# Making the first pair's attention operands on the engines and putting them ahead of the second pair's, in an attention and soft-MoE kernel

## The chip, the core and the metric

One core of a Trainium2 chip. Times are device microseconds (us) of one execution. The core's engines are TensorE (PE, with its weight load PEld), VectorE (DVE), ScalarE (ACT), GpSimd (POOL) and SyncE (SP); ACT, POOL and SP also issue DMAs, which the profile writes as ACTq, POOLq and SPq. All the DMAs run on 16 shared DMA engines.

## The reference

```python
q_n, k_n = rmsnorm(q, g_q), rmsnorm(k, g_k)         # x / sqrt(mean(x*x) + 1e-6) * g, over D = 64
scores = (q_n @ k_n.T) / sqrt(D)                    # 4 batches, 12 heads, 448 rows
attn = softmax(scores) @ v                          # 1792 rows of 768
x = (relu(attn @ w_in) ** 2) @ w_out                # 768 -> 2048 -> 768, weights in 64-bit floats
logits = x @ phi                                    # 8 experts of 4 slots
slot_input = softmax(logits, over rows).T @ x
slot_out[e] = relu(slot_input[e] @ w1[e]) @ w2[e]   # 768 -> 1024 -> 768
out = softmax(logits, over slots) @ slot_out
```

## The kernel before

Attention works on 24 pairs of heads, six to a batch. While it goes on, the 64-bit weights of the first layer are fetched in 32 pieces of 768 KB (`fetch64`, on GpSimd's DMA queue), turned into 32-bit floats on ACT and DVE (`convert`: tiles `top`, `wf`, `wh`), and stored to scratch memory on SP's queue (`wi_s`, `wo_s`); the first layer's products for a finished batch (`ph`) fill TensorE's gaps. After attention come the last batch's first layer and the experts, whose weights SP streams in.

The code is written as blocks (`load`, `norm`, `trans0`, `trans1`, `max0`, `row0`, `s00`, `v00` and so on), which `attention` calls in the sequence of `ORDER`, each with its distance in pairs ahead of the scores. A scheduler then puts every engine's instructions in one fixed order; an engine takes them strictly in that order, and one that waits holds everything behind it on that engine or queue.

What happens to one pair, with the tile names:

- `load` brings q and k of both heads (`qk`). It has four buffers, two per pair, so that the loads of pair 2 wait until pair 0's `norm` has read its own, and those of pair 3 until pair 1's has.
- `norm` squares both on ACT (`sq`, one buffer), sums on DVE (`ss`), makes the inverse root by a first guess on ACT (`y`, L245) and three Newton rounds of three small DVE steps (L247 to L249), and multiplies (`qs`, L261).
- `trans` turns q and k over on TensorE into PSUM (`pm`) and makes the operands of each head. `m1` is q rounded to the matmul format, on 64 partitions, and again on the other 64; `m2` is what the rounding left, and row 64 of `m2` holds minus the row maximum. `s1` is k times the gains `gkq`, rounded, with its residue on the other 64 partitions; `s2` is the rounded part again. ACT writes the rounded halves, DVE the residues, and the two second copies (`m1` to `m1`, `s1` to `s2`) are made by DMA: pair 0's on ACT's queue (`small`), the others' on SP's. The profile cuts numbers off, so that `m<-m` is the copy of `m1`, and `m<-mt` the write of the row maxima.
- `rowmax` multiplies `s1` with `m1` and takes the maximum on DVE (`nm`), `maxrow` turns it over, copies it (`mt`) and sends it by DMA into row 64 of `m2`. `scores` does the two products that make the final scores; of the first pair `s00` and `s01` belong to head 0. `values` multiplies with v (`pv`).

Three sets of `m1`, `m2`, `s1`, `s2` go round among the heads. Ahead of the first pair stand `gains` (the product of g_q, g_k and the scale, one DVE instruction that waits for four small loads on ACT's queue) and, in the code of the same time, `selectors` (constant tiles `i4`, `r4`, `i4h`, `seln`, `sel4`, some 13 small DVE instructions). `gate` is a DVE instruction that holds the first weight conversion back until pair 0's last operand is made.

Of the kernel before, what the change touches and what calls it, by code (L numbers as in the profile page):

```python
# [20 lines left out]
def raw(ap):  # L21
    return ap.bitcast(F32)
# [19 lines left out]
VF, PD, LEAD, SLOPE = 9, 4, 1.5, 0.75  # L42
WF, EARLY, NTOP = 4, 1, 1
LAG, GATE, MTQ = 1, 1, 1


ON_PL = [1, 0, 1, 1, 1, 1, 1, 1, 1, 1, 1, 0, 1, 0, 0, 1]
# [12 lines left out]
def tile_attention_moe_softmoe(  # L60
# [22 lines left out]
    nc = tc.nc  # L83
# [20 lines left out]
    make_identity(nc, ident)  # L104
    gkq = const.tile([128, 1], F32, tag="gkq", name="gkq")
    gq2 = const.tile([128, 1], F32, tag="gq2", name="gq2")
    i4 = const.tile([128, 32], F32, tag="i4", name="i4")
    r4 = const.tile([128, 4, 32], F32, tag="r4", name="r4")
    i4h = const.tile([128, 2, 32], F32, tag="i4h", name="i4h")
# [93 lines left out]
    def load_v(t):  # L203
        b, hp = divmod(t, NP)
        vh, vl = vst[t % 2]
        if t < VF:
            vf = att.tile([CP, 2, NC, D + 1], F32, tag="vr", name=f"vf_{t}", bufs=2)
            nc.vector.memset(vf[:, :, :, D:], 1.0)
            live[t]["vf"] = vf
            for j in range(2):  # L210
                nc.sync.dma_start(
                    vf[:, j, :, :D], v[b, 2 * hp + j].rearrange("(p c) d -> p c d", c=NC)
                )
            return
        vr = att.tile([CP, 2, NC, D + 1], F32, tag="vr", name=f"vr_{t}", bufs=2)
        vr = vr.rearrange("p h c d -> p (h c d)")[:, : 2 * NC * D].rearrange("p (h c d) -> p h c d", h=2, c=NC)
        nc.sync.dma_start(
            vr.rearrange("p h c d -> p h (c d)"),
            v[b, 2 * hp : 2 * hp + 2].rearrange("h (p c) d -> p h (c d)", c=NC),
        )  # L220
        for j in range(2):
            nc.scalar.copy(vh[:, j, :, :D], vr[:, j])
        for j in range(2):
            nc.vector.tensor_tensor(vl[:, j], vr[:, j], raw(vh[:, j, :, :D]), ALU.subtract)
# [6 lines left out]
    def inverse_rms(ts):  # L231
        n = 16 * len(ts)
        ss = att.tile([CP, 32], F32, tag="ss", name=f"ss_{ts[0]}", bufs=1)[:, :n]
        for x, t in enumerate(ts):
            for i in range(2):
                sq = att.tile([CP, 8, D], F32, tag="sq", name=f"sq_{t}_{i}", bufs=1)
                qf = live[t]["qk"][i].rearrange("p h c d -> p (h c) d")
                nc.scalar.activation(sq, qf, AF.Square)  # L238
                at = 16 * x + 8 * i
                nc.vector.tensor_reduce(ss[:, at : at + 8], sq, AX.X, ALU.add)  # L240
        ms = att.tile([CP, 32], F32, tag="ms", name=f"ms_{ts[0]}", bufs=1)[:, :n]
        y = att.tile([CP, 32], F32, tag="y", name=f"y_{ts[0]}", bufs=2)[:, :n]
        u = att.tile([CP, 32], F32, tag="u", name=f"u_{ts[0]}", bufs=1)[:, :n]
        nc.vector.tensor_scalar(ms, ss, 1.0 / D, EPS, ALU.mult, ALU.add)
        nc.scalar.activation(y.bitcast(I32), ms.bitcast(I32), AF.Copy, bias=float(0x5F3759DF), scale=-0.5)  # L245
        for _ in range(3):
            nc.vector.scalar_tensor_tensor(u, y, -0.5, y, ALU.mult, ALU.mult)  # L247
            nc.vector.tensor_tensor(u, u, ms, ALU.mult)
            nc.vector.scalar_tensor_tensor(y, u, 1.5, y, ALU.add, ALU.mult)  # L249
        for x, t in enumerate(ts):  # L250
            live[t]["y"] = y[:, 16 * x : 16 * x + 16]

    def norm(t):
        ts = together(t)
# [20 lines left out]
    def trans(t, i):  # L275
# [6 lines left out]
        for j in range(2):  # L282
            o = operands(t, j)
            src = ps[64 * j : 64 * j + 64, :S]
            if i == 0:
                nc.scalar.copy(o["m1"][0:64, :], src)
                small(t).dma_start(raw(o["m1"][64:128, :]), raw(o["m1"][0:64, :]))
                nc.vector.tensor_tensor(o["m2"][0:64, :], src, raw(o["m1"][0:64, :]), ALU.subtract)
            else:
                g = gkq[64 * j : 64 * j + 64, :]  # L290
                nc.scalar.activation(o["s1"][0:64, :], src, AF.Copy, scale=g)
                small(t).dma_start(raw(o["s2"][0:64, :]), raw(o["s1"][0:64, :]))
                nc.vector.scalar_tensor_tensor(
                    o["s1"][64:128, :], src, g, raw(o["s1"][0:64, :]), ALU.mult, ALU.subtract
                )
                if GATE and t == 0 and j == 1:
                    gate(raw(o["s1"][0:1, 0:1]))
# [5 lines left out]
    def gains():  # L303
        for half in range(2):
            nc.scalar.dma_start(gkq[64 * half : 64 * half + 64, :], g_k.rearrange("(d o) -> d o", o=1))
            nc.scalar.dma_start(gq2[64 * half : 64 * half + 64, :], g_q.rearrange("(d o) -> d o", o=1))
        nc.vector.scalar_tensor_tensor(gkq, gkq, scale, gq2, ALU.mult, ALU.mult)

    def selectors():
        nc.sync.dma_start(phi_sb, phi.rearrange("(kc p) s -> p kc s", p=128))  # L310
        nc.vector.tensor_tensor(i4, ident[:, 0:32], ident[:, 32:64], ALU.add)
        nc.vector.tensor_tensor(i4, i4, ident[:, 64:96], ALU.add)
        nc.vector.tensor_tensor(i4, i4, ident[:, 96:128], ALU.add)
# [122 lines left out]
    def attention():  # L436
        for t in range(-3, NT + 1):
            for key in ORDER:
                dt, cost, run = blocks[key]
                if 0 <= t + dt < NT:  # L440
                    run(t + dt)
                    if t == -3:
                        gains()
                        for u in units[:PD]:
# [697 lines left out]
```

## Time and profile before

| | |
|---|---|
| Median of 3 runs | 835.5 us (829.1, 835.5, 840.67) |
| The profiled execution | 825.38 us, of which the span of its instructions is 823.4 us |
| Granted TensorE clock, mean over the span | 0.973 of 2.4 GHz |
| Busy share of the span | PE 90%, PEld 63%, DVE 61%, ACT 48%, POOL 14% |
| Moved by DMA | 185.22 MB, 225 GB/s |

Rows are read against the span, which begins at 0; 1.98 us of the execution lie outside it. A busy share is a mean over stages that differ: the first 60 us, in which loads come in and the first pairs are made, look nothing like the 400 us in the middle.

### The profile page before, as it was taken

The numbers are of one execution on the slowest core, as the hardware profiler recorded it, in microseconds if no ns is written. First come the engines' busy times: TensorE is split into PE (matmuls) and PEld (weight loads), VectorE is DVE, ScalarE is ACT, GpSimd is POOL, SyncE is SP. The second block draws the span as 40 slices with busy tenths as digits, with TensorE's granted clock in tenths as the row PEclk, the third lists the DMA queues.
The fourth block names the chain that finished last, engine by engine and source line by source line (L and its number), as shares of the span: only waits on it lengthen the run. The fifth ranks groups of instructions, "written<-read, shape, count | busy, mean of one in ns | idle before, by whom it ended". The sixth has DMA issues, their size and how long they took to land.

```text
span 823.4 us, 11533 instructions
## 1 busy us (share of the span) xinstructions
PE 739.0 (90%) x4030; PEld 516.6 (63%) x4030; DVE 500.7 (61%) x954; ACT 392.6 (48%) x664; POOL 117.8 (14%) x113
## 2 busy tenths in 40 slices
PE   0668988899999999999999999999999999998784
PEld 0334654467777887677877858787866887443122
DVE  6578886785588879977687789676336223220013
ACT  2457776665457566566656665555412122120012
POOL 3011010100111210313112323322200000000000
PEclk9989999999999999999999999999999999899997
DMA  8688897857776563345444423433336997999998
GB/s 256 193 293 269 277 264 242 257 184 248 250 243 200 185 197 110 106 129 158 142 145 140 137 79 112 149 101 99 115 120 256 416 415 294 384 415 416 396 339 267
DMA packets 76952, 185.22 MB, mean 225 GB/s; under 512 B 19264, under 2 KB 44384, under 8 KB 76896
## 3 DMA queue, kind: packets, MB, share of 16 engines
q1 hardware_dynamic: 70368, 158.64, 56.0%
q0 software_dynamic: 5632, 25.17, 9.7%
q10 hardware_dynamic: 896, 0.69, 0.3%
q8 instruction: 32, 0.52, 0.3%
q14 instruction: 24, 0.20, 0.1%
HBM read 148.73 MB, written 24.38 MB: 210 GB/s over the span
## 4 chain that ended last, share of the span: by engine, by line
PE 71%; DMA 9%; DVE 6%; ACT 6%; issue 3%; SPq 3%; POOL 0%; ACTq 0%; DVEq 0%; POOLq 0%
PE ph L149 25%; PE pv L149 13%; PE pss L149 12%; PE pm L149 8%; PE pe L149 4%; DMA m<-m 3%; PE pm L651 3%; DMA qk<-in_q_dram 2%; DMA w<-in_moe_w_dram 2%; PE pt L149 1%; PE pm L279 1%; DMA wi_s<-wh 1%; SPq L917 1%; PE so_ps L149 1%; ACT p L356 1%
## 5 line engine op out<-in xcount | busy, mean ns | idle before, releaser
L149 PE MATMUL ph<-xh,whl 128*128 128x448 f32 x900 | 217.4, 373 | 2.3 <-ACT gt L683 1.8
L149 PEld LDWEIGHTS ph<-xh,whl 128*128 128x128 f32 x900 | 165.8, 188 | 23.0 <-ACT gt L683 4.4
L334 DVE TENSOR_REDUCE nm<-pss 112x2 f32<-112x896 f32 x96 | 102.3, 1085 | 17.4 <-PE pss L149 16.5
L356 ACT ACTIVATE p<-pss 112x896 f32<-112x896 f32 x96 | 87.5, 917 | 53.0 <-PE pss L149 52.0
L149 PE MATMUL pss<-m,s 65*112 65x448 f32 (+1 forms) x384 | 109.2, 404 | 2.8 <-ACT p L356 1.5
L149 PEld LDWEIGHTS pss<-m,s 65*112 65x112 f32 (+1 forms) x384 | 68.2, 184 | 26.6 <-DVE nm L334 7.1
L683 ACT ACTIVATE gt<-ph 128x448 f32<-128x448 f32 x64 | 34.8, 543 | 94.1 <-PE ph L149 92.6
L149 PE MATMUL pss<-s,m 128*112 128x448 f32 x192 | 59.6, 411 | 20.9 <-DMA m<-m 14.6
L149 PE MATMUL pv<-p,vf 112*65 112x448 f32 x144 | 69.9, 597 | 4.6 <-ACT p L356 2.7
L149 PE MATMUL pv<-ph,vst 112*65 112x448 f32 x240 | 72.0, 377 | 0.1
L361 DVE TENSOR_TENSOR pl<-p,ph 112x896 fp32r<-112x896 f32 x42 | 47.6, 1133 | 21.4 <-ACT ph L360 20.6
L691 POOL TENSOR_TENSOR gt<-gt 128x448 f32<-128x448 f32 x29 | 30.9, 1067 | 191.4 <-ACT gt L683 159.9
L149 PEld LDWEIGHTS pss<-s,m 128*112 128x112 f32 x192 | 32.4, 183 | 39.2 <-issue 18.6
L360 ACT ACTIVATE ph<-pss 112x896 fp32r<-112x896 f32 x60 | 55.1, 918 | 3.8 <-PE pv L149 3.3
L691 DVE TENSOR_TENSOR gt<-gt 128x448 f32<-128x448 f32 x30 | 19.4, 648 | 58.4 <-ACT gt L683 58.4
L149 PE MATMUL ph<-xh,wi 128*128 128x448 f32 x252 | 54.4, 370 | 0.0
L361 POOL TENSOR_TENSOR pl<-p,ph 112x896 fp32r<-112x896 f32 x18 | 38.2, 2124 | 111.5 <-ACT ph L360 111.5
L149 PEld LDWEIGHTS ph<-xh,wi 128*128 128x128 f32 x252 | 46.5, 188 | 3.9
L240 DVE TENSOR_REDUCE ss<-sq 112x8 f32<-112x512 f32 x48 | 32.5, 678 | 21.9 <-ACT sq L238 21.6
L149 PE MATMUL pv<-pl,vst 112*65 112x448 f32 x120 | 44.7, 372 | 0.4 <-DVE pl L361 0.3
L382 ACT COPY t<-pv 65x448 f32<-65x448 f32 x48 | 25.2, 525 | 40.1 <-PE pv L149 40.1
L238 ACT ACTIVATE sq<-qk 112x512 f32<-112x512 f32 x48 | 30.2, 630 | 28.3 <-DMA qk<-in_q_dram 11.1
(163 smaller groups left out, 1052.7 us busy)
## 6 DMA issues: line engine op xcount, KB each, us to landing
w<-in_moe_w_dram SPq DMA_DIRECT2D x60, 768.0 KB
whl<-wi_s SPq DMA_DIRECT2D x50, 768.0 KB
w<-in_moe_w_in_dram POOLq DMA_DIRECT2D x16, 768.0 KB, 7.1
w<-in_moe_w_out_dram POOLq DMA_DIRECT2D x16, 768.0 KB, 6.8
wi<-wi_s SPq DMA_DIRECT2D x14, 768.0 KB
wi_s<-wh SPq DMA_DIRECT2D x16, 384.0 KB
wi_s<-wf SPq DMA_DIRECT2D x16, 384.0 KB
wo_s<-wf SPq DMA_DIRECT2D x16, 384.0 KB
```

The source lines that it names most:

```text
L149: nc.tensor.matmul(o, lhsT, rhs, start=start, stop=stop)
L238: nc.scalar.activation(sq, qf, AF.Square)
L240: nc.vector.tensor_reduce(ss[:, at : at + 8], sq, AX.X, ALU.add)
L279: nc.tensor.transpose(ps[:, c * CP : (c + 1) * CP], x[:, c].rearrange("p h d -> p (h d)"), ident[:CP, :CP])
L334: nc.vector.tensor_reduce(nm[:, 2 * half : 2 * half + 2], ps[:CP, :, :S], AX.X, ALU.max, negate=True)
L356: nc.scalar.activation(p, ps[:CP, :, :S], AF.Exp)
L360: nc.scalar.activation(ph, ps[:CP, :, :S], AF.Exp)
L361: engine(ON_PL[t // NP * 4 + 2 * j + half]).tensor_tensor(pl, p, raw(ph), ALU.subtract)
L382: nc.scalar.copy(tt[: D + 1, j, :], ps[: D + 1, :S])
L651: nc.tensor.transpose(ps[:CP, fi * 128 : (fi + 1) * 128], gt[fi][:, c * CP : (c + 1) * CP], ident)
L683: nc.scalar.activation(gt, ps[:, :S], AF.Relu, scale=1.0 / UP)
L691: (nc.vector if k else nc.gpsimd).tensor_tensor(gt, gt, gt, ALU.mult)
```

## The change

For pair 0 alone, the two `trans` blocks give way to `trans_first`, called straight behind pair 0's `norm`: the second half of `m1` is copied from PSUM by DVE and `s2` is written by ACT, so that the four DMA copies fall away, and `m2` and `s2` come behind both heads' `m1` and `s1`. Four tiny DVE copies make later work depend on pair 0: pair 1's first square on `qs` of pair 0's k, pair 1's `ms` on the last of pair 0's `s1`, and two selector tiles on the same. The gains' product goes to GpSimd in two instructions; in GpSimd's order the first stands ahead of the small copies that precede the first weight fetches, the second right ahead of those fetches.

```diff
+DUPE, HIP, SELG, VC, AHEAD = 0, 0, 1, 0, 1
...
+    gsc = const.tile([128, 1], F32, tag="gsc", name="gsc")
+    nc.gpsimd.memset(gsc, scale)
...
                 sq = att.tile([CP, 8, D], F32, tag="sq", name=f"sq_{t}_{i}", bufs=1)
+                if AHEAD and t == 1 and i == 0:
+                    nc.vector.tensor_copy(sq[0:1, 0, 0:1], live[0]["qs"][1][0:1, 0, 0, 0:1])
...
+        if AHEAD and ts[0] == 1:
+            nc.vector.tensor_copy(ms[64:65, 0:1], raw(operands(0, 1)["s1"][64:65, 0:1]))
         nc.vector.tensor_scalar(ms, ss, 1.0 / D, EPS, ALU.mult, ALU.add)
...
+    def trans_first():
+        pss = []
+        for i in range(2):
+            ps = mps()
+            x = live[0]["qs"][i]
+            for c in range(NC):
+                nc.tensor.transpose(
+                    ps[:, c * CP : (c + 1) * CP], x[:, c].rearrange("p h d -> p (h d)"), ident[:CP, :CP]
+                )
+            pss.append(ps)
+        for j in range(2):
+            o = operands(0, j)
+            h = slice(64 * j, 64 * j + 64)
+            m, s, g = pss[0][h, :S], pss[1][h, :S], gkq[h, :]
+            nc.scalar.copy(o["m1"][0:64, :], m)
+            nc.vector.tensor_copy(o["m1"][64:128, :], m)
+            nc.scalar.activation(o["s1"][0:64, :], s, AF.Copy, scale=g)
+            nc.vector.scalar_tensor_tensor(o["s1"][64:128, :], s, g, raw(o["s1"][0:64, :]), ALU.mult, ALU.subtract)
+        if GATE:
+            gate(raw(o["s1"][64:65, 0:1]))
+        for j in range(2):
+            o = operands(0, j)
+            h = slice(64 * j, 64 * j + 64)
+            nc.vector.tensor_tensor(o["m2"][0:64, :], pss[0][h, :S], raw(o["m1"][0:64, :]), ALU.subtract)
+            nc.scalar.activation(o["s2"][0:64, :], pss[1][h, :S], AF.Copy, scale=gkq[h, :])
...
-        nc.vector.scalar_tensor_tensor(gkq, gkq, scale, gq2, ALU.mult, ALU.mult)
+        if SELG:
+            nc.gpsimd.tensor_tensor(gkq, gkq, gq2, ALU.mult)
+            nc.gpsimd.tensor_tensor(gkq, gkq, gsc, ALU.mult)
...
+        if SELG:
+            behind = raw(operands(0, 1)["s1"][64:68, 0:2])
+            nc.vector.tensor_copy(i4[64:68, 0:2], behind)
+            nc.vector.tensor_copy(seln, behind)
...
+                if AHEAD and t + dt == 0 and key in ("trans0", "trans1"):
+                    pass
...
+                    if AHEAD and t + dt == 0 and key == "norm":
+                        trans_first()
```

The other new switches (`DUPE`, `HIP`, `VC`) are 0 and do nothing. How the fixed order of the engines changes is seen at three places. The tile names keep a number for the buffer here, and the line numbers of the changed kernel are larger.

VectorE before, from the gains' product into pair 0's normalisation (`ss_160` is pair 0's, `ss_189` pair 1's):

```order
L307 SCALAR_TENSOR_TENSOR gkq<-gkq,gq_64 128x1
L240 TENSOR_REDUCE ss_160<-sq_0_161 112x8
L240 TENSOR_REDUCE ss_160<-sq_1_164 112x8
L244 TENSOR_SCALAR ms_167<-ss_160 112x16
L240 TENSOR_REDUCE ss_189<-sq_0_190 112x8
L247 SCALAR_TENSOR_TENSOR u_169<-y_168 112x16
L311 TENSOR_TENSOR i_65<-ident 128x32
L320 TENSOR_TENSOR seln<-ident 4x2
L248 TENSOR_TENSOR u_169<-u_169,ms_167 112x16
```

VectorE with the change, from the same place:

```order
L252 TENSOR_REDUCE ss_163<-sq_0_164 112x8
L252 TENSOR_REDUCE ss_163<-sq_1_167 112x8
L258 TENSOR_SCALAR ms_170<-ss_163 112x16
L261 SCALAR_TENSOR_TENSOR u_172<-y_171 112x16
L262 TENSOR_TENSOR u_172<-u_172,ms_170 112x16
L263 SCALAR_TENSOR_TENSOR y_171<-u_172,y_171 112x16
```

The gains' product has left VectorE, and neither pair 1's sum nor a selector stands among pair 0's Newton steps any more.

ScalarE before, from the first pair's operands on (`m_0_109` and `m_1_114` are the two heads' `m1`, `s_0_111` and `s_1_116` their `s1`, `s_0_112` and `s_1_117` their `s2`; `qk_0_185` is pair 2's q):

```order
L286 CAST m_0_109<-pm_214 64x448
L287 DMA m_0_109<-m_0_109 64x448
L291 ACTIVATE s_0_111<-pm_225,gkq 64x448
L286 CAST m_1_114<-pm_214 64x448
L292 DMA s_0_112<-s_0_111 64x448
L287 DMA m_1_114<-m_1_114 64x448
L238 ACTIVATE sq_0_316<-qk_0_185 112x512
L291 ACTIVATE s_1_116<-pm_225,gkq 64x448
L292 DMA s_1_117<-s_1_116 64x448
```

ScalarE with the change, from pair 0's first guess on (`m_0_111`, `m_1_116` the two `m1`, `s_0_113`, `s_1_118` the two `s1`, `s_0_114`, `s_1_119` the two `s2`; `qk_0_159` and `qk_1_161` are pair 1's q and k, `qk_0_211` pair 2's q, `y_224` pair 1's first guess):

```order
L250 ACTIVATE sq_0_216<-qk_0_159 112x512
L282 CAST m_0_111<-pm_188 64x448
L284 ACTIVATE s_0_113<-pm_193,gkq 64x448
L250 ACTIVATE sq_1_220<-qk_1_161 112x512
L282 CAST m_1_116<-pm_188 64x448
L284 ACTIVATE s_1_118<-pm_193,gkq 64x448
L250 ACTIVATE sq_0_323<-qk_0_211 112x512
L292 ACTIVATE s_0_114<-pm_193,gkq 64x448
L292 ACTIVATE s_1_119<-pm_193,gkq 64x448
L553 ACTIVATE top_135<-w_1_147 128x768
L259 ACTIVATE y_224<-ms_223 112x16
```

The four DMA copies are gone. The square of pair 2's q stood between the two heads' operands and now stands behind both, with the two `s2`, the first conversion and pair 1's first guess behind it.

VectorE before, from the gate to the second head's row maxima (`nm_0_237` is head 0's maximum, `nm_1_246` head 1's, `mt` the copies for row 64 of `m2`):

```order
L301 TENSOR_SCALAR top_133<-s_1_116 1x1
L334 TENSOR_REDUCE nm_0_237<-pss_238 112x2
L334 TENSOR_REDUCE nm_0_237<-pss_242 112x2
L334 TENSOR_REDUCE nm_1_246<-pss_247 112x2
L334 TENSOR_REDUCE nm_1_246<-pss_251 112x2
L342 CAST mt_0_257<-pm_255 4x112
L491 SCALAR_TENSOR_TENSOR wf_278<-w_1_144,top_133 128x768
L342 CAST mt_1_262<-pm_260 4x112
```

VectorE with the change, from the copy that ties pair 1's `ms` to pair 0 (`nm_0_242` and `nm_1_251` are the two heads' maxima, `u_225` and `y_224` pair 1's Newton steps):

```order
L257 COPY ms_223<-s_1_118 1x1
L389 TENSOR_REDUCE nm_0_242<-pss_243 112x2
L258 TENSOR_SCALAR ms_223<-ss_215 112x16
L389 TENSOR_REDUCE nm_0_242<-pss_247 112x2
L261 SCALAR_TENSOR_TENSOR u_225<-y_224 112x16
L389 TENSOR_REDUCE nm_1_251<-pss_252 112x2
L262 TENSOR_TENSOR u_225<-u_225,ms_223 112x16
L389 TENSOR_REDUCE nm_1_251<-pss_256 112x2
L263 SCALAR_TENSOR_TENSOR y_224<-u_225,y_224 112x16
L397 CAST mt_0_262<-pm_260 4x112
```

Pair 1's Newton steps, which ran before pair 0's last operands, now alternate with pair 0's row maxima. Further on, on VectorE, `qs` of pair 1 stands as row 60 and 61 where it stood as 47 and 48, behind the copies of both heads' maxima, one weight conversion and half of the selectors; on TensorE pair 1's transposes stand behind the scores of pair 0's head 0, where they stood ahead of them.

## Rows read from the trace of the kernel before

**Rows 1.** Windows: busy us (count) of PE, PEld, DVE, ACT, POOL; clock; DMA; GB/s.

```profile
0.00:60.00 60.00, 26.35 (x76) 14.95 (x77) 38.12 (x97) 23.30 (x36) 9.09 (x22) 0.94 0.82 253
60.00:200.00 140.00, 123.49 (x581) 80.23 (x580) 107.25 (x204) 93.88 (x153) 13.72 (x20) 0.95 0.78 242
200.00:620.00 420.00, 414.12 (x2219) 318.73 (x2218) 305.55 (x548) 241.41 (x398) 92.30 (x69) 1.00 0.47 150
```

**Rows 2.** Chain that ended last, in order of time: start, us, what.

```profile
18.56 10.22 DMA m<-m
...
45.85 7.87 DMA wi_s<-wh
```

**Rows 3.** Timeline, 0 to 20 us: start, us, engine, line, operation, count, idle before.

```profile
5.13 0.63 ACT L238 ACTIVATE sq<-qk 112x512 f32<-112x512 f32 x1
...
6.70 2.65 POOL L476 DMA_DIRECT2D w<-in_moe_w_in_dram  x3
7.63 0.16 DVE L307 SCALAR_TENSOR_TENSOR gkq<-gkq,gq 128x1 f32<-128x1 f32 x1 [4.28 <-DMA vf<-in_v_dram]
7.71 0.68 DVE L240 TENSOR_REDUCE ss<-sq 112x8 f32<-112x512 f32 x1
...
14.31 1.29 DVE L261 TENSOR_TENSOR qs<-qk,y 112x512 f32<-112x512 f32 x2
...
15.08 0.33 SPq L196 DMA_DIRECT2D qk<-in_q_dram  x1
...
15.14 1.73 PE L279 MATMUL pm<-ident,qs 112*128 112x112 f32 x8 [15.14 <-DVE qs L261]
...
16.16 0.53 ACT L286 CAST m<-pm 64x448 fp32r<-64x448 f32 x1 [1.55 <-PE pm L279]
16.35 0.17 DVE L248 TENSOR_TENSOR u<-u,ms 112x16 f32<-112x16 f32 x1
16.56 0.17 DVE L249 SCALAR_TENSOR_TENSOR y<-u,y 112x16 f32<-112x16 f32 x1
...
16.86 0.61 DVE L288 TENSOR_TENSOR m<-pm,m 64x448 fp32r<-64x448 f32 x1
17.32 0.63 ACT L291 ACTIVATE s<-pm,gkq 64x448 fp32r<-64x448 f32 x1 [0.64 <-PE pm L279]
...
19.77 0.68 DVE L293 SCALAR_TENSOR_TENSOR s<-pm,gkq,s 64x448 fp32r<-64x448 f32 x1
```

**Rows 4.** Timeline, 24 to 42 us.

```profile
24.48 1.80 PE L149 MATMUL pss<-s,m 128*112 128x448 f32 x4 [7.62 <-DMA m<-m]
24.83 0.63 ACT L238 ACTIVATE sq<-qk 112x512 f32<-112x512 f32 x1 [6.32 <-DMA qk<-in_q_dram]
...
27.09 2.09 DVE L334 TENSOR_REDUCE nm<-pss 112x2 f32<-112x896 f32 x2
...
29.70 1.05 ACT L490 ACTIVATE top<-w 128x768 f16<-128x768 bf16 x1
...
32.30 1.84 ACTq L343 DMA_DIRECT2D m<-mt  x2
...
32.67 1.71 PE L279 MATMUL pm<-ident,qs 112*128 112x112 f32 x8
...
34.20 2.55 PE L149 MATMUL pss<-m,s 65*112 65x448 f32 x6
...
36.64 3.25 PE L149 MATMUL pv<-p,vf 112*65 112x448 f32 x4
...
39.57 0.61 ACT L291 ACTIVATE s<-pm,gkq 64x448 fp32r<-64x448 f32 x1
```

**Rows 5.** Page, costliest groups: a GpSimd product; busy us, mean ns, idle before.

```profile
L691 POOL TENSOR_TENSOR gt<-gt 128x448 f32<-128x448 f32 x29 | 30.9, 1067 | 191.4 <-ACT gt L683 159.9
```

**Rows 6.** DMA queues from 18 to 21 us: packets, MB, share of 16 engines.

```profile
q0 software_dynamic: 213, 0.90, 83.2%
q1 hardware_dynamic: 150, 0.15, 17.1%
```

More of the change, by code (lines that the diff above doesn't have):

```diff
@@ L44 @@
 LAG, GATE, MTQ = 1, 1, 1
+DUPE, HIP, SELG, VC, AHEAD = 0, 0, 1, 0, 1
+FIRST = "load norm trans0 trans1 max0 max1 row0 row1 s00 s01 s10 s11".split()
 ON_PL = [1, 0, 1, 1, 1, 1, 1, 1, 1, 1, 1, 0, 1, 0, 0, 1]
@@ L209, in load_v @@
             live[t]["vf"] = vf
+            if VC:
+                vr = att.tile([CP, 2, S], F32, tag="pl", name=f"vr_{t}", bufs=2)[:, :, : NC * D]
+                nc.sync.dma_start(vr, v[b, 2 * hp : 2 * hp + 2].rearrange("h (p c) d -> p h (c d)", c=NC))
+                nc.gpsimd.tensor_copy(vf[:, :, :, :D], vr.rearrange("p h (c d) -> p h c d", c=NC))
+                return
             for j in range(2):
@@ L286, in trans @@
                 nc.scalar.copy(o["m1"][0:64, :], src)
-                small(t).dma_start(raw(o["m1"][64:128, :]), raw(o["m1"][0:64, :]))
+                if t < DUPE:
+                    nc.scalar.copy(o["m1"][64:128, :], src)
+                else:
+                    small(t).dma_start(raw(o["m1"][64:128, :]), raw(o["m1"][0:64, :]))
                 nc.vector.tensor_tensor(o["m2"][0:64, :], src, raw(o["m1"][0:64, :]), ALU.subtract)
@@ L291, in trans @@
                 nc.scalar.activation(o["s1"][0:64, :], src, AF.Copy, scale=g)
-                small(t).dma_start(raw(o["s2"][0:64, :]), raw(o["s1"][0:64, :]))
+                if t < DUPE:
+                    nc.vector.tensor_scalar(o["s2"][0:64, :], src, g, None, ALU.mult)
+                else:
+                    small(t).dma_start(raw(o["s2"][0:64, :]), raw(o["s1"][0:64, :]))
                 nc.vector.scalar_tensor_tensor(
@@ L306, in gains @@
             nc.scalar.dma_start(gq2[64 * half : 64 * half + 64, :], g_q.rearrange("(d o) -> d o", o=1))
-        nc.vector.scalar_tensor_tensor(gkq, gkq, scale, gq2, ALU.mult, ALU.mult)
+        if SELG:
+            nc.gpsimd.tensor_tensor(gkq, gkq, gq2, ALU.mult)
+            nc.gpsimd.tensor_tensor(gkq, gkq, gsc, ALU.mult)
+        else:
+            nc.vector.scalar_tensor_tensor(gkq, gkq, scale, gq2, ALU.mult, ALU.mult)
     def selectors():
         nc.sync.dma_start(phi_sb, phi.rearrange("(kc p) s -> p kc s", p=128))
+        if SELG:
+            behind = raw(operands(0, 1)["s1"][64:68, 0:2])
+            nc.vector.tensor_copy(i4[64:68, 0:2], behind)
+            nc.vector.tensor_copy(seln, behind)
         nc.vector.tensor_tensor(i4, ident[:, 0:32], ident[:, 32:64], ALU.add)
@@ L439, in attention @@
                 dt, cost, run = blocks[key]
+                if AHEAD and t + dt == 0 and key in ("trans0", "trans1"):
+                    pass
+                elif 0 <= t + dt < HIP and key in FIRST:
+                    with tc.high_priority(offset=0):
+                        run(t + dt)
+                elif 0 <= t + dt < NT:
+                    run(t + dt)
                 if 0 <= t + dt < NT:
-                    run(t + dt)
+                    if AHEAD and t + dt == 0 and key == "norm":
+                        trans_first()
                     if t == -3:
```

## The prediction

> **What bounds the kernel now.** I began with the busy time by stage [rows 1]. From 200 to 620 us TensorE is busy 414.12 of 420 us: there only less TensorE work, or an earlier start, can shorten the kernel. From 60 to 200 us it is busy 123.49 of 140, and in the first 60 us only 26.35 of 60. The 33.65 us that it idles there are where this change works; it takes nothing from TensorE's own work. Next I read the chain that ended last: in the first 60 us its longest pieces are the DMA copy of `m1`, 10.22 us, and a store of a converted weight, 7.87 us [rows 2]. The timeline then shows the start step by step. TensorE's first instruction comes at 15.14 us, released by `qs`; its first product `s1` by `m1` comes at 24.48, after 7.62 us of waiting for the DMA copies [rows 3, 4]. Ahead of them VectorE waits until 7.63 us for the gains, though ACT had its first square ready at 5.13 + 0.63 = 5.76 [rows 3].
>
> **The change part by part.** I follow pair 0 in the new order, with durations from the rows and the hand-over between engines as the timeline shows it (0.05 to 0.2 us).
>
> Normalisation. The first sum begins at 5.8 instead of 7.71, a gain of 1.9. Sum 0.68, second square 0.63, second sum 0.68 and two 16-element steps bring the Newton rounds to 8.4. Nine steps at 16.56 - 16.35 = 0.21 each, with nothing between them, end at 10.3; the two products `qs` of 0.65 (1.29 for two) end at 11.6. Before, they began at 14.31 [rows 3]. So this step gives 4.0 us: 1.9 for the gains, 2.1 for pair 1's sums and the selectors, which go behind.
>
> Operands. The first four transposes take until 16.16 - 15.14, one us after their start [rows 3]: PSUM is ready at 12.1. In ACT's new order a square of pair 1 stands first, held until both `qs` are done: 11.75 to 12.4. Then `m1` 0.53 and `s1` 0.63 end at 13.6. VectorE's second half of `m1` is new; the nearest row is the residue `m2` from the same PSUM shape, 0.61, bounded below by ACT's 0.53 and above by the 0.68 of `s1`'s residue [rows 3], so 0.1 us either way. With that residue, head 0 is complete at 14.45 and its products begin at 14.6 instead of 24.48: **9.9 us earlier**. Head 1 follows: ACT until 15.45, VectorE until 16.5, then two `m2`, the gate and a tie, until 17.9. The row maxima begin there, not at 27.09 [rows 4].
>
> The Trainium skill's page "DMA: Bandwidth & Descriptors" (section "Anatomy of one DMA") gives a DMA some 2.0 us plus its bytes at 436 GB/s. By that the 112 KB copies would take an estimated 2.3 us, and the removed wait would be worth far less than the 9.9 us; the copy on the chain took 10.22 us [rows 2], so the trace disagrees here and the measurement stands.
>
> Where the head start goes. Behind head 1's operands ACT now takes the square of **pair 2's q**, and behind that both `s2`, the first weight conversion and pair 1's first guess `y`. The load of that q is issued when `qs` frees its buffer, at 11.1 instead of 15.08; before, it was there at 24.83, 9.75 us after its issue [rows 3, 4]. The reason shows in the queues: from 18 to 21 us the weight fetches (q0) held 83.2% of the DMA engines and SP's queue (q1) got 150 packets, 50 per us [rows 6]. At that pace 224 KB in 1 KB packets take 4.5 us; the other 5 of the 9.75 are start and completion. Without pair 0's copies on ACT's queue I take a little less, 8.8 us, a landing at 19.9; the bounds are 24.8 (it comes no earlier than before) and 16.6 (from which on other things bind). Until then ACT waits 4.4 us.
>
> After that landing: square 0.63, two `s2` 1.26, `top` 1.05 and the guess 0.2 end at 23.2. VectorE has done both maxima of head 0 by 20.2 and stands at pair 1's first Newton step, which needs that guess; head 1's maxima and even head 0's copy `mt` are queued behind. Two maxima of 1.05 and two steps later `mt` is done at 26.0, and its DMA is issued at 26.05 instead of 32.30. At most 34.20 - 32.30 = 1.9 us later it lands, and head 0's scores run from 28.0, 2.5 us long, to 30.5. Before, they began at 34.20 [rows 4], so 6.2 us of the head start are left.
>
> Pair 1. Its eight transposes, 1.71 us, lay free in the wait for the row maxima [rows 4]; now they come behind the scores and are paid. Their `qs` come, after `mt` of head 1 at 26.45, behind a conversion of 0.95, some 13 small steps (0.17 busy each [rows 3], but most do not depend on the one before and overlap; 0.1 is my estimate), a sum of 0.68 and the products' 1.3: done at 30.5, just in time. The transposes end at 32.2, and the first product with v starts then instead of 36.64 [rows 4]: **4.4 us earlier**. This is what I expect of the start.
>
> Pair 3. Its loads wait for pair 1's `qs` and go from 18.5 to 30.0. Few other loads are then under way; between the 1.9 us of the row maxima's small DMA and the 9.75 of pair 2's load I take 4, so 34.0, when ACT has waited 1.3 us in front of pair 1's own operands. These end at 35.8 instead of 39.57 + 0.61 = 40.2 [rows 4]: still 4.4 earlier. If the load takes the 9.75 us of pair 2's, the lead is lost here (below).
>
> The gains on GpSimd. Two instructions on 128 x 1; GpSimd's product over 448 columns took 1.07 us [rows 5], VectorE's over one 0.16 [rows 3], and I take 0.2. The gains land by 7.6 and are first read at 13.0, so that even 1.07 each costs nothing there. What is queued behind on GpSimd is the weight fetches: they go from 6.70 to between 8.2 and 10. The first conversion asks for its weight at about 21.9, and before it ran at 29.70 with its fetch from 6.70, so that 3 us less of lead is covered. The late fetches leave SP's queue freer until 10 us. The selectors are 1.3 us of VectorE moved behind pair 0's maxima, half of it ahead of pair 1's `qs`, counted above.
>
> From there on the work is the same. The profiled execution would go from 825.38 to 821.0. The median of the runs shown lies 10.1 us above that execution, for no reason that a trace shows; I put the same 4.4 us against it: 835.5 - 4.4 = 831.
>
> **The rivals.** First, **more of the head start is kept**. If the load of pair 2's q lands before 16.6, ACT does not wait, pair 1's guess is there at 19.4, VectorE never stands, and `mt` goes out at 23.05, 3 us earlier than I have it; the first product with v starts at 29.1, 7.5 us earlier than before: 828. For it: GpSimd's fetches start later, and the copies are gone. Against it: the 9.75 us of the same load. The Trainium skill's page "DMA: Bandwidth & Descriptors" (section "Anatomy of one DMA") is on this rival's side: by its rule the load would take an estimated 2.5 us; that row disagrees. Second, **the lead is used up by DMA**. Between 60 and 200 us TensorE idles 16.5 us and DMA is at 0.78, in the first 60 us at 0.82 [rows 1]; the store of 7.87 us at 45.85 [rows 2] holds ACT. If the weight stream sets the pace there, the lead ends in a longer wait: 835.5, no change. Against it: the fetches and stores are released by conversions, which come earlier too, and 448 KB of copies are taken away.
>
> Third, on the other side, **ACT waits for both loads**. If pair 2's q lands at 24.8 as before, everything from there is 4.9 us later than in my sum: the products with v start 0.5 us later than before, and pair 3's loads go out at 34.9. If these take 9.75 us as well they land at 44.65 and pair 1's operands end at 46.5, 6.3 us later than before: 842. The point from which the kernel becomes slower is a landing of pair 2's q at 24.3, or of pair 3's q 8.3 us or more after its issue at 30.0. Against it: the weight fetches in flight then are fewer, since GpSimd's next ones wait for conversions. Fourth, **the whole head start is kept, and more**: 9.9 us and the 7.87 us of the store on the chain, if it is out of the way by then, give 835.5 - 17.8 = 818. The trace shows no reason for the second part. That the change does not do what it says I leave out: in the new order the copies and the gains are gone from the first pair's path.
>
> **How the numbers follow.** Forecast, 831: 0.46. More kept, 828: 0.22. Used up by DMA, 835.5: 0.15. Both loads late, 842: 0.10. All kept and more, 818: 0.07. The runs before spread by 829.1 to 840.67, and a new median may move by some 5 us. The range reaches from 828 less 7 to 835.5 plus 6, or **821 to 841**; the two outer cases are left out in part. A measurement of this kernel tells about 2%, or 16.7 us, from no change: only the fourth rival is faster by that, 0.08, and nothing above is slower by it; with a schedule that falls badly later on I leave that 0.04. The rest, 0.88, is within 2%.
>
> **What would show it.** Right: first sum near 5.8 us, first product `s1` by `m1` near 14.6, ACT idle before the square of pair 2's q, VectorE idle before pair 1's first Newton step, `mt` out near 26, products with v near 32. Then the clock and idle time after 60 us stay as before. Wrong: the loads of pair 2 or 3 at other times than 19.9 and 34.0; a new wait of TensorE after 40 us; or an order of later pairs that costs more than the start brings.

## The result, and the profile after

| | before | changed |
|---|---|---|
| Median of four executions each | 833.0 us (829.1 to 840.67) | 818.98 us (817.02 to 822.19) |
| Ratio, with 95% interval | | 0.986 [0.982, 0.990] |
| A later comparison, 17 and 6 executions (e10) | 831.33 us | 821.42 us, ratio 0.988 [0.985, 0.992] |
| Profiled execution, span | 825.38, 823.4 us | 818.53, 816.3 us |

The change makes the kernel faster by 10 to 12 us, 1.2 to 1.4%, within the 2% bound. The sign of the forecast was right and its size was not: 4.4 us were forecast. The first median, 818.98, lies 2 us below the stated range of 821 to 841, and the later one, 821.42, just inside it; taken from the 835.5 that the forecast started from, the ratio 0.986 gives 823.7. (The ratios leave out executions that lie far above the fastest of their kernel, three of ten in e5, four of ten in e7 and two at most in the other kernels; below the ratios are used.)

The windows of the changed kernel, with the columns of [rows 1]:

```profile
0.00:60.00 60.00, 31.77 (x113) 18.72 (x113) 44.10 (x114) 30.26 (x48) 10.79 (x27) 0.97 0.83 270
60.00:200.00 140.00, 121.67 (x572) 81.28 (x571) 105.43 (x196) 92.61 (x149) 12.29 (x18) 0.94 0.79 243
200.00:620.00 420.00, 415.04 (x2223) 319.33 (x2222) 308.21 (x558) 238.47 (x394) 90.22 (x69) 1.00 0.46 146
```

In the first 60 us TensorE does 113 instructions where it did 76, and idles 28.23 us where it idled 33.65. Behind that the stages read as before. The timeline of the changed kernel, 5 to 36 us, answers [rows 3, 4]:

```profile
5.78 0.69 DVE L252 TENSOR_REDUCE ss<-sq 112x8 f32<-112x512 f32 x1 [2.43 <-ACT sq L250]
...
7.55 0.19 POOL L355 TENSOR_TENSOR gkq<-gkq,gq 128x1 f32<-128x1 f32 x1 [5.84 <-DMA vf<-in_v_dram]
...
10.24 1.29 DVE L302 TENSOR_TENSOR qs<-qk,y 112x512 f32<-112x512 f32 x2
11.01 0.33 SPq L200 DMA_DIRECT2D qk<-in_q_dram  x1
...
13.17 0.62 DVE L283 CAST m<-pm 64x448 fp32r<-64x448 f32 x1
...
14.43 1.84 PE L153 MATMUL pss<-s,m 128*112 128x448 f32 x4 [1.63 <-DVE s L285]
...
18.14 1.09 DVE L389 TENSOR_REDUCE nm<-pss 112x2 f32<-112x896 f32 x1
...
20.18 0.63 ACT L250 ACTIVATE sq<-qk 112x512 f32<-112x512 f32 x1 [4.94 <-DMA qk<-in_q_dram]
...
23.28 0.18 DVE L261 SCALAR_TENSOR_TENSOR u<-y 112x16 f32<-112x16 f32 x1 [2.85 <-ACT y L259]
...
25.83 1.90 ACTq L398 DMA_DIRECT2D m<-mt  x2
...
27.60 2.58 PE L153 MATMUL pss<-m,s 65*112 65x448 f32 x6 [1.28 <-DMA m<-mt]
...
29.06 1.27 DVE L302 TENSOR_TENSOR qs<-qk,y 112x512 f32<-112x512 f32 x2
...
29.80 0.31 SPq L200 DMA_DIRECT2D qk<-in_q_dram  x1
...
31.47 2.92 PE L153 MATMUL pv<-p,vf 112*65 112x448 f32 x4
...
34.26 0.63 ACT L250 ACTIVATE sq<-qk 112x512 f32<-112x512 f32 x1 [1.71 <-DMA qk<-in_q_dram]
...
35.21 0.63 ACT L335 ACTIVATE s<-pm,gkq 64x448 fp32r<-64x448 f32 x1
```

The idle times in brackets are the new waits: ACT 4.94 us for pair 2's q, VectorE 2.85 for the first guess `y` that stands behind it on ACT. Read against the prediction's steps:

| Step | Forecast | Measured |
|---|---|---|
| First sum begins | 5.8 | 5.78 |
| Pair 0's `qs` done | 11.6 | 11.53 |
| First product `s1` by `m1` | 14.6 | 14.43 |
| Row maxima begin | 17.9 | 18.14 |
| Pair 2's q issued, there | 11.1, 19.9 | 11.01, 20.18 |
| Pair 1's guess done | 23.2 | 23.25 |
| `mt` goes out | 26.05 | 25.83 |
| Scores of head 0 begin | 28.0 | 27.60 |
| Pair 1's `qs` done | 30.5 | 30.33 |
| First product with v | 32.2 | 31.47 |
| Pair 3's q issued, there | 30.0, 34.0 | 29.80, 34.26 |
| Pair 1's first `s1` done | 35.8 | 35.84 |

No step is off by more than 0.8 us. What differs from the forecast lies behind this start.

### The profile page after: what moved, and what is told of

It is laid out like the page before. It is cut to its first block, busy times and chain, and to the rows that moved or that the text cites. A ratio compares the mean times of both kernels' runs of the same rounds, so it can differ in the third digit from the quotient of the medians.

```text
span 816.3 us, 11544 instructions
## 1 busy us (share of the span) xinstructions
PE 735.7 (90%) x4030; PEld 517.0 (63%) x4030; DVE 502.0 (61%) x959; ACT 394.6 (48%) x666; POOL 116.0 (14%) x116
## 4 chain that ended last, share of the span: by engine, by line
PE 73%; DMA 7%; ACT 4%; DVE 4%; SPq 3%; issue 1%; DVEq 0%; ACTq 0%
PE ph L153 27%; PE pv L153 13%; PE pss L153 12%; PE pm L153 7%; PE pe L153 4%; PE pm L714 3%; DMA m<-m 3%; DMA w<-in_moe_w_dram 2%; PE pm L320 1%; SPq L980 1%; PE pt L153 1%; PE so_ps L153 1%; SPq L977 1%; DMA wi_s<-wh 1%; ACT p L411 1%
## 5 line engine op out<-in xcount | busy, mean ns | idle before, releaser
L153 PE MATMUL pss<-s,m 128*112 128x448 f32 x192 | 61.6, 418 | 18.5 <-DMA m<-m 6.0
L153 PE MATMUL pv<-p,vf 112*65 112x448 f32 x144 | 67.3, 582 | 2.5 <-ACT p L411 2.5
L754 POOL TENSOR_TENSOR gt<-gt 128x448 f32<-128x448 f32 x29 | 28.7, 991 | 195.8 <-ACT gt L746 187.8
L252 DVE TENSOR_REDUCE ss<-sq 112x8 f32<-112x512 f32 x48 | 32.4, 675 | 17.5 <-ACT sq L250 17.2
```

Of the source, the lines that this page charges most:

```text
L153: nc.tensor.matmul(o, lhsT, rhs, start=start, stop=stop)
L754: (nc.vector if k else nc.gpsimd).tensor_tensor(gt, gt, gt, ALU.mult)
```

## The experiments

The line numbers of a variant's rows are its own, close to those of the changed kernel. One quantity recurs: the **lead**, by which a profiled execution reaches its first product with v ahead of 36.04 us, the mean of the two profiles of the kernel before (36.64 and 35.43). The changed kernel has 4.57, and 5.07 in e10.

### How far two runs of one kernel differ

**e1_before_again**: the kernel before, no edit.

> The kernel before, unchanged, to see a second execution of it in the profile. If the runs above 829 us lose their time at the start (the copies of the first operands come later in some executions than in others), the first product s1 by m1 moves away from 24.5 us and the first product with v from 36.6, by as much as the span moves from 823.4. If they lose it elsewhere, both stay within 1 us and the span moves all the same. Median expected 829 to 838.

Measured: 831.2 us (825.79 to 841.58), ratio 0.999 [0.995, 1.003]. Its profile reaches the first product with v 1.2 us earlier than the other profile of the same kernel, and ends 1.2 us later. So one profile places the start to about a microsecond; and the executions spread over 16 us, far more than the starts of the two profiles differ. Neither profile is of one of the longer executions, so where those lose their time stays open.

**e10_after_again**: the changed kernel, no edit.

> The changed kernel once more, without a difference, with more executions. If the 12 us between the medians are the change's, the median lies at 817 to 821 and the ratio at 0.982 to 0.989. If the four executions were lucky ones, and the other kernels of this set (823 to 830 with nearly the same start) show what such an order gives in the mean, it lies at 823 to 827.

Measured: 821.42 us (820.39 to 822.16), ratio 0.988 [0.985, 0.992]. The gain is the change's; it is nearer 10 than 12 us.

### The parts of the change

**e8_engine_copies_only**: the copies on the engines, everything else as before (the kernel's own switch for them; ACT writes the second `m1`, VectorE makes `s2`).

```diff
-DUPE, HIP, SELG, VC, AHEAD = 0, 0, 1, 0, 1
+DUPE, HIP, SELG, VC, AHEAD = 1, 0, 0, 0, 0
```

> The kernel before with nothing but the first pair's second copies made by ScalarE (m1) and VectorE (s2): gains on VectorE, selectors and pair 1 in their former places. Theory (the copies and the order are worth little apart): first product s1 by m1 at 19 to 21, but pair 2's square still stands between the two heads on ScalarE and its load lands at 23 to 25, so head 1's products come at 26 to 28 and the first product with v at 34 to 36; span 820 to 823. Rival (the copies alone are the gain): first product with v at 31.5 to 32.5, span 816 to 818.

Measured: 835.75 us, ratio 1.002 [0.998, 1.007]. From its timeline:

```profile
14.76 1.73 PE L320 MATMUL pm<-ident,qs 112*128 112x112 f32 x8 [14.76 <-DVE qs L302]
...
23.42 0.63 ACT L250 ACTIVATE sq<-qk 112x512 f32<-112x512 f32 x1 [5.93 <-DMA qk<-in_q_dram]
...
25.18 0.63 DVE L332 TENSOR_TENSOR m<-pm,m 64x448 fp32r<-64x448 f32 x1 [5.88 <-ACT m L329]
25.82 0.68 DVE L340 SCALAR_TENSOR_TENSOR s<-pm,gkq,s 64x448 fp32r<-64x448 f32 x1
...
26.64 1.80 PE L153 MATMUL pss<-s,m 128*112 128x448 f32 x4 [10.16 <-DVE s L340]
```

Without the new order the copies' removal gains nothing: the square of pair 2's q still stands among the first pair's operands on ACT, waits 5.93 us for its load, and holds them. The first product comes at 26.64, later than the 24.48 of [rows 4], with VectorE where the DMA stood as what released it. It was expected at 19 to 21; but on VectorE the residue of head 0's `s1` (25.82) stands behind head 1's `m2` (25.18), and so behind that load as well.

**e4_copies_by_dma**: the changed kernel with the second copies made by DMA again.

```diff
-            nc.vector.tensor_copy(o["m1"][64:128, :], m)
+            nc.scalar.dma_start(raw(o["m1"][64:128, :]), raw(o["m1"][0:64, :]))
...
-            nc.scalar.activation(o["s2"][0:64, :], pss[1][h, :S], AF.Copy, scale=gkq[h, :])
+            nc.scalar.dma_start(raw(o["s2"][0:64, :]), raw(o["s1"][0:64, :]))
```

> The changed kernel in its order, with the four second copies made by DMA on ScalarE's queue again. Theory (the copies cost because they share the DMA engines with the weight fetches): issued at 13 us, they land 7 to 8 us later; first product at 20 to 22 instead of 14.4, head 1's 2 us after that; then pair 2's load no longer matters; first product with v at 33 to 35, span 818 to 820. By the Trainium skill's page 'DMA: Bandwidth & Descriptors' (section 'Anatomy of one DMA') the copies would take an estimated 2.3 us. Rival (a copy costs about 2 us): first product at 16, first product with v at 31.5, span 816.

Measured: 828.44 us, ratio 0.997 [0.995, 1.000]. Its timeline:

```profile
12.86 0.51 ACTq L283 DMA_DIRECT2D m<-m  x1
...
20.33 1.81 PE L153 MATMUL pss<-s,m 128*112 128x448 f32 x4 [7.53 <-DMA m<-m]
...
33.76 1.47 PE L153 MATMUL pv<-p,vf 112*65 112x448 f32 x2
```

The order alone brings the copy's issue to 12.86 us, and TensorE then waits 7.53 us for it: 5.9 us at the first product, 2.3 at the first product with v. So at the start order and copies need each other. Of the 7.5 us that this copy took, the first 4.3 went by without a packet on ACT's queue (q10), which is missing from the queues of 12.9 to 17.2 us:

```profile
q0 software_dynamic: 370, 1.40, 94.8%
q1 hardware_dynamic: 97, 0.10, 7.9%
```

The Trainium skill's page "DMA: Bandwidth & Descriptors" (section "Anatomy of one DMA") gives a fit for DMAs that GpSimd issues; carried over to a copy of this size it would be an estimated 2.3 us, and the trace disagrees.

**e3_gains_selectors_only**: gains on GpSimd and selectors tied, the rest as before.

```diff
-DUPE, HIP, SELG, VC, AHEAD = 0, 0, 1, 0, 1
+DUPE, HIP, SELG, VC, AHEAD = 0, 0, 1, 0, 0
```

> Only the gains on GpSimd and the selectors behind; the first pair's operands by DMA copies and in the former order. Theory: the copies are issued 2 us earlier, but still wait behind the weight fetches, and pair 2's square again stands between the two heads on ScalarE: first product s1 by m1 at 22 to 24, first product with v at 34.5 to 36, span 821 to 823. Rival (the order and the gains are what counts, not the copies): first product with v at 32 to 33, span 817 to 819.

Measured: 829.16 us, ratio 0.996 [0.992, 1.000]; first transposes at 12.33 us, first product 21.57 after 7.51 us for the copy, first product with v 33.60.

**e2_gains_selectors_back**: the changed kernel with the gains on VectorE and the selectors free.

```diff
-DUPE, HIP, SELG, VC, AHEAD = 0, 0, 1, 0, 1
+DUPE, HIP, SELG, VC, AHEAD = 0, 0, 0, 0, 1
```

> The changed kernel with the gains' product on VectorE again and the selectors where they were. Theory (each step of the first pair's path is worth what it measures): first sum back at 7.7 us, qs 3.2 us later than in the changed kernel, the load of pair 2's q issued 3 us later, and since everything waits for that load, the first product with v at 34 to 35 instead of 31.5; span 818.5 to 820. Rival (the waiting load hides the difference, the weight fetches start 1.8 us earlier and that is what counts): product with v at 31.5 to 32.5, span 815 to 817.

Measured: ratio 0.993 [0.989, 0.997]; first product 16.89 us, first product with v 35.35. The two steps together are worth 2.5 us at the first product and 3.9 at the first product with v.

**e11_gains_only**: the changed kernel with the selectors free, gains on GpSimd.

```diff
-        if SELG:
+        if 0:
             behind = raw(operands(0, 1)["s1"][64:68, 0:2])
```

> The changed kernel, but the selectors are not tied to the last of pair 0's operands, so that the scheduler puts them where it had them, among pair 0's Newton steps on VectorE; the gains' product stays on GpSimd. It parts the two things that e2 put back together (823.6). If the gains carry that difference: first sum at 5.8 us, first product near 15.2, 819 to 820. If the selectors do: first product 0.7 to 1.3 us later than 14.43, and 822 to 824.

Measured: 820.36 us, ratio 0.987 [0.983, 0.992]; first product 15.79, first product with v 33.42. The selectors among the Newton steps cost 1.4 us at the first product and 2 at the first product with v, and nothing that the medians show. That leaves the difference between e2 and the changed kernel to the gains; the intervals of e2 and e11 overlap, so for the time this is not shown.

### Where the lead goes

**e6_load_at_start** and, once more, **e12_load_at_start_again**: the changed kernel with pair 2's q and k in buffers of their own, so that they load at once and ACT does not wait for them.

```diff
-            x = att.tile([CP, 2, NC, D], F32, tag="qk", name=f"qk_{t}_{i}", bufs=4)
+            if t == 2:
+                x = att.tile([CP, 2, S], F32, tag="pl", name=f"qk_{t}_{i}", bufs=2)
...
+            else:
+                x = att.tile([CP, 2, NC, D], F32, tag="qk", name=f"qk_{t}_{i}", bufs=4)
```

> The changed kernel with pair 2's q and k in two other buffers that are free at the start, so that their loads go out at once and pair 3's when pair 0's qs is done. Theory: no wait of ScalarE for either load (4.9 and 1.7 us in the changed kernel), first product with v at 28.5 to 29.5, pair 1's operands done at 32 to 33 instead of 35.8; the loads of v and the weight fetches come up to 1.5 us later, which is covered; span 812 to 815. Rival (the DMA engines are the limit of the start, so a load moved ahead costs what is behind it): pair 0's own operands or the first conversion come later, product with v at 31 to 33, span 816 to 818.

> The kernel of e6 once more (pair 2's q and k in buffers of their own, loaded at once), with more executions: ACT does not wait for pair 2's q, but the write of the row maxima comes out just as late. If that wait was worth the 3 us which the first rival of the prediction had for it, the median lies 3 us under that of the changed kernel in the same set; if the small DMA and the clock take it back, as e6 looked, it lies within 1.5 us of it.

Measured: 819.28 us (816.37 to 826.3), ratio 0.985 [0.978, 0.992]; and 816.72 us (813.88 to 824.94), ratio 0.984 [0.979, 0.989]. From e12's timeline:

```profile
22.99 1.90 ACTq L402 DMA_DIRECT2D m<-mt  x2
...
27.83 2.58 PE L153 MATMUL pss<-m,s 65*112 65x448 f32 x6 [4.35 <-DMA m<-mt]
...
31.70 1.91 PE L153 MATMUL pv<-p,vf 112*65 112x448 f32 x4
...
35.62 0.73 PE L153 MATMUL pss<-s,m 128*112 128x448 f32 x2
```

The row maxima go out 2.8 us earlier, and arrive no earlier: 27.83 against 27.60. The queues differ: the weight fetches (q0, the software queue) fill them in one and not in the other. First e12 from 23 to 27.8 us; packets, MB, share of the 16 engines:

```profile
q0 software_dynamic: 305, 1.53, 89.9%
...
q10 hardware_dynamic: 16, 0.00, 0.4%
```

Then the changed kernel from 25.8 to 27.6 us, where q10, ACT's queue, is the only one:

```profile
q10 hardware_dynamic: 8, 0.00, 0.5%
```

The same 1.8 KB took 4.84 us beside a weight fetch and 1.77 on idle DMA engines; in e12 no packet of q10 moved before 25.5 us. The earlier load does pay further on, since TensorE starts pair 1's first products at 35.62 instead of 40.84 us. Whether this variant beats the changed kernel is not settled: e6's ratio is 0.001 lower than that of the first comparison and e12's 0.004 lower than e10's, with intervals that overlap. Its two profiles differ by 7.0 us of span (818.7 and 811.7), of which 4.7 arise in one place. Windows of e6, 690 to 710 us, then of e12, columns as above:

```profile
690.00:700.00 10.00, 8.59 (x44) 4.41 (x44) 4.48 (x14) 1.87 (x5) 1.80 (x1) 0.63 0.97 377
700.00:710.00 10.00, 10.00 (x90) 4.89 (x89) 0.89 (x2) 0.80 (x3) 0.00 (x0) 0.86 0.80 293
```

```profile
690.00:700.00 10.00, 9.99 (x95) 5.45 (x84) 3.24 (x6) 0.80 (x3) 1.80 (x1) 1.00 1.02 420
700.00:710.00 10.00, 8.93 (x81) 4.46 (x80) 0.91 (x2) 1.34 (x3) 0.00 (x0) 1.00 1.02 414
```

In e6 TensorE was granted 0.63 and then 0.86 of its clock there, in e12 all of it. From 695 to 700 us e6 stood at 0.50, the lower of the two levels (1.2 GHz). The same products, first in e6 and then in e12:

```profile
691.81 2.91 PE L153 MATMUL pm<-gn,en 112*32 112x512 f32 x16 [0.47 <-DVE en L804]
```

```profile
689.38 1.92 PE L153 MATMUL pm<-gn,en 112*32 112x512 f32 x16 [0.47 <-DVE en L804]
```

Ahead of them TensorE had idled for 0.47 us, and a little earlier for 1.03, in both runs alike, so these rows do not tell why the clock fell in one. The two windows of e6 lack (1 - 0.63) x 10 + (1 - 0.86) x 10 = 5.1 us of full clock, about what it lost. From the 11th to the 21st load of expert weights, issued between 675 and 707 us, e6 took 28.7 us and e12 24.0. Over the 14 profiles this stretch is 24.0 (seven), 25.6 (two) or 28.7 to 28.8 (five): a step of up to 4.8 us that the same kernel may or may not take.

**e5_square_later**: the changed kernel with pair 2's first square tied behind pair 1's last Newton step.

```diff
+                if AHEAD and t == 2 and i == 0:
+                    nc.vector.tensor_copy(sq[0:1, 0, 0:1], live[1]["y"][0:1, 0:1])
```

> The changed kernel with one more tiny VectorE copy that ties the first square of pair 2 to pair 1's finished inverse root, so that on ScalarE it stands behind both s2, the first conversion, pair 1's first guess and pair 0's first softmax. Theory (ScalarE's wait for pair 2's load, 4.9 us, is what took back part of the head start): pair 1's first guess at 19.4 instead of 23.1, mt out at 23 instead of 25.8, first product with v at 28.5 to 29.5 instead of 31.5; span 813 to 815, if the lead goes through to the end. Rival (what comes after 60 us takes up any lead): same product with v, span 816 to 818.

Measured: 828.83 us, ratio 0.993 [0.988, 0.998]. No other run has its first product with v as early, at 30.29, with `mt` out at 23.11. Yet by the ratio it gains 4 us less than e10, with intervals that overlap.

**e7_both**: the edits of e5 and e6 together.

> Both edits at once: pair 2's square later and its loads at the start. Theory: no better than the better of the two alone by more than 1 us at the first product with v, since each removes the same wait; pair 3's load is out of the way as well; span 812 to 815. Rival: the two gains add, first product with v at 26 to 27, span 809 to 811.

Measured: 829.78 us, ratio 0.993 [0.988, 0.998]; `mt` out at 23.04, first product with v at 31.15. Again an early start with little to show for it.

**e9_start_delayed**: the changed kernel with a later start. Pair 0's first square is done nine times; the extra work has no effect on the output, and no other instruction changes its place on any engine.

```diff
                 nc.scalar.activation(sq, qf, AF.Square)
+                for _ in range(8 if t == 0 and i == 0 else 0):
+                    nc.scalar.activation(sq, qf, AF.Square)
```

> The changed kernel, with pair 0's first square done nine times instead of once, 8 x 0.63 = 5.04 us of ACT's idle time; every engine's order is otherwise that of the changed kernel, and the weight fetches are not delayed. So the first sum begins at 10.8 us, the first product near 19.5, and the first product with v near 36 instead of 31.47, where the kernel before had it (36.64). Theory A, the lead at the first products with v is carried one for one: 819.0 + 5 = 824, and the other 7 of the 12 us between the medians come from the order behind the start. Rival B, the whole gain hangs on the start: 831. Rival C, a lead at the start does not count, because the weight stream or the later order sets the pace from 60 us on: 819 to 820.

Measured: ratio 0.994 [0.990, 0.997], against 0.988 [0.985, 0.992] of e10 on the same chip. Its timeline:

```profile
5.79 5.26 ACT L252 ACTIVATE sq<-qk 112x512 f32<-112x512 f32 x8
11.07 0.69 DVE L254 TENSOR_REDUCE ss<-sq 112x8 f32<-112x512 f32 x1 [7.72 <-ACT sq L252]
...
19.71 1.83 PE L153 MATMUL pss<-s,m 128*112 128x448 f32 x4 [1.63 <-DVE s L287]
...
35.62 2.83 PE L153 MATMUL pv<-p,vf 112*65 112x448 f32 x4
```

The first product with v is 4.65 us later than in e10, and the ratio is 0.0055 higher, or 4.6 us. That fits theory A, by which a lead at the start is carried to the end one for one, though the two intervals leave some 4 us either way. But at 35.62 us this kernel has almost no lead over the one before (0.42), and is still some 5 us faster, with an interval that excludes no gain. That part of the gain is not in the lead at the first product with v. In its one profile the lead is 2.0 us at pair 12's first row maximum, near 310 us, 2.3 at the 11th expert load and 5.5 at the 21st, behind the stretch at 700 us.

### The runs side by side

The gain is one less the ratio, times the 831.5 us of the kernel before (the median of its executions in all comparisons); its uncertainty is 2 to 4 us, in e6 6. "Order" tells whose fixed order TensorE has behind the start: before's or the changed kernel's. TensorE's orders in these two are the same from row 1016 of 3404 on, at about 296 us, and differ in many small places ahead of it, mostly in which gaps the products of converted weights (`ph`, and `pm` from `phi_sb`) fill. "Stretch" is the time in the profiles from the end of pair 0's second output copy `t`, near 59 us, to the end of pair 12's first row maximum, near 312, which holds most of the rows that differ.

| Run | Order behind the start | Lead | Gain | Gain less lead | Stretch |
|---|---|---|---|---|---|
| before, e1 | before's | -0.6, 0.6 | e1: 0.6 | 0.0 | 253.2, 253.1 |
| e8 | before's | -1.7 | -1.7 | 0.0 | 260.0 |
| e3 | before's | 2.4 | 3.4 | 1.0 | 261.8 |
| e5 | before's from row 334 on | 5.8 | 5.8 | 0.0 | 259.7 |
| e4 | a third, to row 1002 | 2.3 | 2.2 | -0.1 | 264.4 |
| e9 | changed | 0.4 | 5.2 | 4.8 | 254.6 |
| changed kernel, first comparison | changed | 4.6 | 11.7 | 7.1 | 256.0 |
| e10 | changed | 5.1 | 9.7 | 4.6 | 257.5 |
| e2 | changed from row 268 on | 0.7 | 5.6 | 4.9 | 252.9 |
| e11 | changed from row 268 on | 2.6 | 10.6 | 8.0 | 255.4 |
| e6, e12 | changed from row 348 on | 4.2, 4.3 | 12.7, 13.2 | 8.5, 8.9 | 252.5, 252.2 |
| e7 | changed from row 348 on | 4.9 | 5.7 | 0.8 | 259.2 |

Rows 268 and 348 are reached at about 119 and 143 us in the changed kernel. By the ratios the gain follows the lead with before's order, and lies some 5 us or more above it with the changed kernel's, in all runs but e7. The profiles agree in part: those of the kernels with 4.6 us or more above their lead took 252.2 to 257.5 us in the stretch, e7, e8, e3, e5 and e4 259.2 to 264.4. Against it stand the two profiles of the kernel before, which are as fast there in its own order; their executions lie 5 to 6 us below its median. The clock has a share in this too: from 60 to 250 us the mean granted clock was 0.96 in both of these, and 0.93, 0.93 and 0.92 in e8, e3 and e4. And by the medians of all their executions e5 and e7 gain only 3.1 and 2.1 us. So e9 shows that some gain comes beside the lead; that the order behind the start brings it is the likeliest reading, and not shown. No run changes that order alone. All spans expected of e2 to e8 were too short, by 0.5 us in e2 to 13 in e3, whose profile is its slowest execution.

## Why the prediction was right and where it failed

**The start.** All of it held. The gains' 1.9 us and the 2.1 us of other work among the Newton steps: `qs` done at 11.53 against 11.6. The 9.9 us at the first product: 14.43 instead of 24.48, 10.05. Its two halves, which the prediction added up on one path, are not separate gains: e8 shows the copies worth nothing without the order, e4 the order worth a fifth of the measured gain without the copies. VectorE's copy of `m1` took 0.62 us against the 0.61 taken, the GpSimd steps 0.19 and 0.18 against 0.2, where the product of [rows 5] took 1.07.

**Where the head start goes.** The two waits came where they were put: ACT 4.94 us (4.4), VectorE 2.85 for `y`. The load of pair 2's q took 9.17 us (8.8), and its split into 4.5 us of transfer and 5 of "start and completion" fits in size too. In the first 4.3 us after its issue, from 11 to 15.3 us, SP's queue (q1) moved no packet and the weight fetches had the engines:

```profile
q0 software_dynamic: 392, 1.50, 99.6%
```

Then the load came in, in 4.9 us, and from 16 to 20 us the two queues moved the same number of packets:

```profile
q0 software_dynamic: 256, 1.21, 84.5%
q1 hardware_dynamic: 255, 0.24, 20.9%
```

So it is no fixed start and completion: it goes with the weight fetches that were under way. Pair 3's load, beside a single fetch, moved its first packet within 1.5 us, had 63.5% of the engines and took 4.46 us (forecast 4). The forecast's pace of 50 packets per us is partly luck, a mean over a window [rows 6] in which q1 moved nothing for the first 0.7 us; while it moved, it moved some 64 to 68.

**The transposes paid behind the scores, pair 3's loads, pair 1's operands.** Right to within 0.8 us. The lead at the first product with v is 5.2 us between the two profiles, 4.6 to 5.1 against the mean of two; 4.4 were forecast.

**"From there on the work is the same."** The work is the same, its order is not: a start with other instructions in other places let the scheduler place the fillers otherwise on TensorE until about 296 us. In the profiles the step held all the same as far as the expert loads: the two of the changed kernel lead the two of the kernel before by 4.8 us at the first product with v and by 4.7 at the 11th expert load, near 680 us. But by e9 some 5 us come beside the lead, and they were no term of the sum. Which of the moved rows would bring them I could not tell.

**"I put the same 4.4 us against" the median.** This is the step that failed. The forecast took the 10 us between the profiled execution and the median for a constant, and with it the lead for the whole gain. The changed kernel's profiled executions lie within about 1 us of its median (818.53 and 820.39 against 818.98 and 821.42), the two of the kernel before 5 to 6 us below its 831.5. So of the 10 us, the profiles show 6.5 (their means, 825.97 and 819.46). Of these 4.7 are there by the 11th expert load; 3.2 more come by the 21st, where both profiles of the changed kernel took 24.0 us and those of the kernel before 25.6 and 28.8, with a granted clock of 0.66 and 0.51 from 700 to 705 us; and some 1.4 are lost again behind it. The same kernel may or may not meet that lower clock, as e6 and e12 show, so these 3.2 us are not shown to be the change's. The other 3.5 are in executions without a profile, and their cause stays open. The mean granted clock does not tell: over the executions counted its median is 0.971 in the kernel before, and 0.972 and 0.966 in the two comparisons of the changed one.

**The rivals.** *More of the head start is kept*, 828, had the load of pair 2's q as its condition. It did not land early in the changed kernel; where e6 and e12 let it, `mt` went out at 23.0 as that rival said (23.05), and the small DMA took the 3 us back by 27.8. *Used up by DMA* is excluded by the ratio. *Both loads late* failed at its conditions: 20.18 against 24.3, and 4.46 us against 8.3. *All kept and more*, 818, is near the first median by luck: neither the whole 9.9 us was kept, nor the store's 7.87. (The sum on the 2% bound has this rival at 0.08, the list of chances at 0.07.)

## What to carry to other kernels

Where a scheduler sets the order, an edit at the start has two effects, the lead that it makes and a new order of what follows; here the second may have been as large as the first. Compare the engines' orders over the whole program, not only at the edit, and widen the range by what other orders of the same work have given. A lead read from one profile is not yet a gain of the median: how far profiles lie from the median is to be measured for both kernels, as e1 and e10 do. To part the two, delay the start without moving an instruction, as e9 does. A copy moved from DMA to an engine gains nothing while the instruction that waits for the next load still stands ahead of it.

## What the runs showed of the hardware

- A DMA of 1.8 KB from ACT's queue took 1.77 us on idle DMA engines and 4.84 beside a fetch on GpSimd's queue that held 89.9% of them: freeing the issue 2.8 us earlier gained nothing.
- Beside GpSimd's weight fetches a load on SP's queue moved nothing for 4.3 us after its issue, while the fetches moved 392 packets, and then every second packet: 255 against 256 from 16 to 20 us. A copy on ACT's queue in e4 waited 4.3 us for its first packet in the same way. Why the first microseconds went to the other queues alone no run here shows. The 224 KB load took 9.17 us there, and 4.46 where its queue had 63.5%.
- The load's packets are small, 0.24 MB in 255 against 1.21 MB in 256 of the fetches, so that half of the packets were 17% of the bytes. The Trainium skill's page "DMA: Bandwidth & Descriptors" (section "Queues, rings and completion order") says that a DMA engine takes a packet from each queue in turn, by which the size of the packets sets the share of the bytes; from 16 to 20 us the trace agrees. No run here changes the packet size of a load.
- From 695 to 700 us the same kernel was granted 0.50 of TensorE's clock in e6 and 1.00 in e12. Sixteen products took 2.91 us against 1.92 there, and the stretch of ten expert loads around it 28.7 us against 24.0.
